# AdaLN transformer block, forward and backward: every DMA transpose replaced by TensorE transposes, dS of a group's second and fourth unit through the dP ring

## The chip, the cores and the metric

One core of a Trainium2 chip runs the whole program. The metric is the device time of one execution in microseconds. Three executions of the kernel before the change gave 2509.86, 2512.61 and 2517.3 us, so the median is 2512.61 us.

## The reference, cut to what matters

The function is one transformer block whose two layer norms are modulated by a conditioning vector, and the reference returns the output and the gradient of nine inputs.

```
mod = silu(c) @ w_mod                     # six rows: sa, ca, ga, sb, cb, gb
h   = layernorm(x) * (1 + ca) + sa
q, k, v = (h @ wqkv), 32 heads of 16
p   = softmax(q k^T / 4);  o = p v        # 2048 x 2048 scores for each head
x1  = x + ga * (o @ wo)
h2  = layernorm(x1) * (1 + cb) + sb
out = x1 + gb * (relu(h2 @ w1 + b1)^2 @ w2 + b2)
grads = vjp(out)(grad_out)                # for x, wqkv, wo, w1, b1, w2, b2, c, w_mod
```

There are 2048 tokens, 512 features, 1792 hidden units, all inputs in bf16. In the backward pass each head needs dP = dO v^T, dS = p * (dP - rowsum), and from dS the gradients dK = dS^T q and dQ = dS k. With keys on one axis of a tile and queries on the other, one of these two products needs dS as it was made and the other needs it turned. That turned dS is the subject of the larger part of the change.

## The kernel before, in words

Time runs through five stages, and the names below are those of the code.

**Forward attention** (`phase_fwd`, 0 to about 980 us). The outer loop runs over `order`: four chunks of 512 queries, eight groups of four heads, two pairs in a group, so 64 pairs (`n`), and inside each over 16 blocks of 128 keys (`kb`). One step makes two score tiles of 128x512 on TensorE (line 388), one exp of 128x1024 on ScalarE (line 391), and eight small products with V (line 322). Beside that, a `Background` object deals out other TensorE work in small portions. A generator yields a number, which is the cost of what it has just issued in units of one 512-column matmul, or a pair such as `("wait", 3)`, which makes the next three steps deal out nothing, so that another engine has time to finish. `step(rate)` gives about 1.2 units per step in the first chunk of queries and 1.14 in the later ones. `until(mark)`, `take` and `drain` run the generators at once: there the waits are passed over. During the first chunk of queries the background is `gen_qkv` (projections for the next head groups, with `gen_fm` and `gen_vt`, which also bring Q, K and V into token-major or padded layouts by DMA transposes at lines 646 and 705); during the other three it is `gen_mlp` (output projection, the MLP forward and backward of the preceding chunk of 512 tokens, then `gen_do`), with DMA transposes at lines 1176, 1178, 1201, 1248 and 1332, and those of the weights at 1139, 1152 and 1153. `bg.until(g + 1)` and `bg.until(-(g + 1))` in the first chunk, and `bg.until(f"fc2_{SC - 2}")` at line 410 after the loop, force what is not yet done.

**Last chunk and weight gradients** (`last_chunk`, about 983 to 1166 us). The last 512 tokens go through the MLP without attention beside it, and `gen_dw1` and `gen_dw2` make the gradients of w1 and w2 in 14 blocks (`ft`) each. `turned` fetches a block of 12 x 128 columns turned, by DMA (lines 946 and 950), three blocks ahead with four buffers.

**Backward attention** (`attn_bwd`, about 1166 to 2382 us). There are 16 pairs of heads, for each four chunks `c` of 512 keys, for each 16 blocks `ib` of 128 queries: 1024 units. Four units are a group, with `i` from 0 to 3. A unit makes two score tiles (line 1608) in the PSUM ring `st` and two dP tiles (line 1522) in the ring `dp`; each ring has three buffers of one bank. The matmuls of both use 64 rows of the array each, and on opposite halves. ScalarE turns scores into `pu` by exp (line 1611), VectorE multiplies dP by `pu` into `ds` (line 1526). In 160 of the 256 groups the second half of unit `i == 1` is copied to SBUF by ScalarE (line 1540) and multiplied by GpSimd (line 1541) instead. `kv` (line 1459) takes dK and dV from `ds` and `pu` in four column tiles; `dq` (line 1484) takes dQ from `dsT`, the turned dS. `dS` (line 1543) starts, when the fourth unit of a group is done, one DMA transpose of the whole group, at line 1549, on SyncE's queue; for one group in four `turn_ds` (line 1556) first turns four of its 32 blocks on TensorE, and ScalarE copies those out. `dq` runs more than eight pending steps behind (`len(pendq) > 2 * G`). In this stage the order of TensorE, SyncE and GpSimd is the order of the code. GpSimd issues the loads of the next group's tensors (line 1597).

**Last products** (`phase6`, about 2382 us to the end). dK, dQ and dV of all heads are multiplied with the weights; `load_a` (line 1733) turns two token blocks of three tensors by three DMA transposes for each of eight steps.

Of the kernel before, what the change touches and what calls it, by code (L numbers as in the profile page):

```python
# [19 lines left out]
P = 128  # L20
# [85 lines left out]
class K:  # L106
# [160 lines left out]
    def phase_fwd(self):  # L267
# [145 lines left out]
        nc.sync.dma_start_transpose(self.gT_l[:], self.io["grad_out"][0, S - 512:, :])  # L413
# [210 lines left out]
    def gen_fm(self, ps, t, g, s0, dst=None, masked=None):  # L624

        nc = self.nc
        DT, NQ = self.DT, self.NQ
        eb = self.qkv_eb
        pt = ps.tile([P, 512], F32, name="pps")
        for kt in range(DT):  # L630
            nc.tensor.matmul(pt[:], lhsT=self.wpads[t][:, kt, g, :] if g else self.wpad0[t][:, kt, :], rhs=self.xm1T[:, kt, s0:s0 + 512],
                             start=(kt == 0), stop=(kt == DT - 1))
            if kt < DT - 1:
                yield 1
        if dst is None:
            ev = eb.tile([P, 512], BF16, name="ev_fm")
            dst = ev[:]
        nc.vector.tensor_copy(dst, pt[:])
        if masked:
            for j in range(4):  # L640
                (nc.scalar.copy if j == 1 else nc.vector.tensor_copy)(masked[j][32 * j:32 * j + 32, :], ev[32 * j:32 * j + 32, :])
        nc.sync.dma_start((self.QTq_d, self.KTq_d)[t][g, :, s0:s0 + 512], dst)

        def token_major():
            tm = eb.tile([P, 4, 4, 32], BF16, name="ev_tm")
            nc.sync.dma_start_transpose(tm[:].rearrange("p s j e -> p s (j e)"), dst)
            if t:
                nc.gpsimd.dma_start(self.ktm_d[g, :, s0:s0 + 512], tm[:].rearrange("p s j e -> p (s j e)"))
                return
            tmc = eb.tile([P, 4, 4, DH], BF16, name="ev_tmc")  # L650
            nc.gpsimd.tensor_copy(tmc[:], tm[:, :, :, 0:DH])
            w = 4 * DH
            nc.gpsimd.dma_start(self.qtm_d[g, :, s0 // P * w:(s0 // P + 4) * w],
                                tmc[:].rearrange("p s j d -> p (s j d)"))

        if self.late is None:
            token_major()
        else:
            self.late.append(token_major)
        yield 1  # L660

    def gen_qkv(self, kp):
# [3 lines left out]
        for g in range(1, NQ):  # L666
# [8 lines left out]
            if 3 < g <= 3 + self.DT:  # L675
                wt = self.qkv_eb.tile([P, 3 * self.DT, P], BF16, name="wm_t", bufs=1)
                nc.sync.dma_start_transpose(wt[:], w[:])
                nc.gpsimd.dma_start(self.WmT_d[g - 4], wt[:].rearrange("p n k -> p (n k)"))
# [14 lines left out]
    def gen_vt(self, s0):  # L693
# [4 lines left out]
        for k in range(4):  # L698
# [6 lines left out]
            nc.sync.dma_start_transpose(vT[:, :, k * P:(k + 1) * P], vp[:].rearrange("p g j e -> p (g j e)"))  # L705
            yield ("wait", 1)
        nc.gpsimd.dma_start(self.VTq_d.rearrange("g p s -> p g s")[:, :, s0 * P:(s0 + 4) * P], vT[:])

# [53 lines left out]
    def last_chunk(self, bg, O_b, x0s, o32):  # L762
# [11 lines left out]
        tps = self.open_pool("tps", bufs=2, space=PSUM)  # L774
# [25 lines left out]
        bg.take(4)  # L800
        stats = mk.tile([P, 4, 6], F32, name="stats")
# [137 lines left out]
    def turned(self):  # L939

        nc, ST, FT = self.nc, self.ST, self.FT
        lasts = []

        def get(pool, src, src_d, ft):
            r = pool.tile([P, ST - 4, P], BF16, name="tm_blk", bufs=4)
            nc.sync.dma_start_transpose(r[:], src_d[ft, :, :(ST - 4) * P])
            if ft % 4 == 0:
                n = min(4, FT - ft)
                t = pool.tile([P, 4, 4, P], BF16, name="tm_l", bufs=2)
                nc.sync.dma_start_transpose(t[:, :n].rearrange("p f s k -> p (f s) k"),  # L950
                                            src[:, ft:ft + n, :].rearrange("p f k -> p (f k)"))
                lasts.append(t)
            return [r[:, st, :] for st in range(ST - 4)] + [lasts[-1][:, ft % 4, i, :] for i in range(4)]

        return get

    def gen_dw1(self, sb, xh2, duT):
# [22 lines left out]
        dus = [turned(sb, duT, self.duT_d, ft) for ft in range(3)]  # L980
# [3 lines left out]
        for ft in range(FT):  # L984
            if ft + 3 < FT:
                dus.append(turned(sb, duT, self.duT_d, ft + 3))
# [37 lines left out]
    def gen_dw2(self, sb, g_tm, aT, tb):  # L1024
# [15 lines left out]
        load(0)  # L1040
        load(1)
        yield 0
        load(2)
        for ft in range(FT):
            if ft + 3 < FT:
                load(ft + 3)
# [74 lines left out]
    def gen_weights_1(self):  # L1121
# [17 lines left out]
        nc.sync.dma_start_transpose(self.wogaT[:].rearrange("p a b c -> p (a b) c"), wo[:].rearrange("p a b -> p (a b)"))  # L1139

    def gen_weights_2(self):
# [10 lines left out]
        nc.sync.dma_start_transpose(self.W2gbT[:].rearrange("p a b c -> p (a b) c"), w2[:].rearrange("p a b -> p (a b)"))  # L1152
        nc.sync.dma_start_transpose(self.W1mT[:].rearrange("p a b c -> p (a b) c"), w1[:].rearrange("p a b -> p (a b)"))
# [14 lines left out]
    def gen_mlp(self, sc, O_b):  # L1168
# [5 lines left out]
        x_v, g_v, out_v = tm_v(io["A_x"][0]), tm_v(io["grad_out"][0]), tm_v(io["out_0"][0])  # L1174
        OT = mk.tile([P, 4, DT, P], BF16, name="fT", bufs=2)
        nc.sync.dma_start_transpose(OT[:].rearrange("p a b c -> p (a b) c"), O_b[:].rearrange("p a b -> p (a b)"))
        gT = mk.tile([P, DT, 512], BF16, name="fT", bufs=2)
        nc.sync.dma_start_transpose(gT[:], io["grad_out"][0, s0:s0 + 512, :])
        yield ("wait", 9 if sc else 14)
# [21 lines left out]
        nc.sync.dma_start_transpose(xhT[:].rearrange("p a b c -> p (a b) c"), xh[:].rearrange("p a b -> p (a b)"))  # L1201
# [30 lines left out]
        for k in range(4):  # L1232
# [15 lines left out]
            nc.sync.dma_start_transpose(dxT[:], dxb[:])  # L1248
# [40 lines left out]
    def gen_do(self, sc, k, dxT, pads=None, o32=None):  # L1289
# [42 lines left out]
        nc.sync.dma_start_transpose(self.dOTq[:, :, c0:c0 + P], dOpad[:].rearrange("p g j e -> p (g j e)"))  # L1332
# [98 lines left out]
    def attn_bwd(self):  # L1431
# [18 lines left out]
        pend, pendq, turnq, two = [], [], [], []  # L1450
# [92 lines left out]
        def dS(u):  # L1543

            (T, g, jp, c, ib, kvT, pu, dsg, i, grp) = u
            pend.append((T, g, jp, c, ib, kvT, pu, dsg[:, i]))
            if i == G - 1:
                dsT, n = grp
                nc.sync.dma_start_transpose(dsT.rearrange("p (b k) -> p b k", k=P)[:, n:, :],
                                            dsg[:].rearrange("p i a k -> p (i a k)")[:, n * P:])  # L1550
# [4 lines left out]

        def turn_ds(dsg, grp, skip, late):

            dsT = next(t for t in dT_free if not late or t is not own)
            dT_free[:] = [t for t in dT_free if t is not dsT]
            grp.extend((dsT, 0 if skip else 4))  # L1560
            if skip:
                return
            tp = stp.tile([P, 4, P], BF16, name="st")
            for b in range(4):
                nc.tensor.transpose(tp[:, b, :], dsg[:, 0, 0, b * P:(b + 1) * P], self.ident[:])
            nc.scalar.copy(dsT[:, 0:4 * P], tp[:].rearrange("p b k -> p (b k)"))
# [5 lines left out]
        for g in range(NQ):  # L1572
            for jp in range(2):
# [16 lines left out]
                for c in range(SC):  # L1590
                    c0 = 512 * c
                    for ib0 in range(0, ST, G):
# [6 lines left out]
                        for i in range(G):  # L1599
# [21 lines left out]
                            elif i % 2 == 0 and len(pendq) > 2 * G:  # L1621
                                for _ in range(4 if end else 2):
                                    dq(pendq.pop(0))
                            if i == 2:
                                turn_ds(dsg, grp, no_turn(c, ib), end and m > 2)
            T = Tn
        with tc.manual_schedule(engines=ALL):
# [5 lines left out]
            dS(last)  # L1633
            while len(pend) > 2:
# [50 lines left out]
    def phase6(self):  # L1685
# [47 lines left out]
        def load_a(i):  # L1733
            s2 = order[2 * i]
            dqT = wk.tile([P, 3, 2, DT, P], BF16, name="dqT", bufs=3)
            for t in (1, 2, 0):
                nc.sync.dma_start_transpose(dqT[:, t].rearrange("p s n k -> p (s n) k"),
                                            parts[t][:, s2:s2 + 2, :].rearrange("p s d -> p (s d)"))
# [227 lines left out]
```

## Time and profile before

| what | value |
|---|---|
| median of three executions | 2512.61 us |
| the profiled execution, its own time | 2500.32 us |
| its span | 2498.5 us |
| granted TensorE clock, mean | 0.998 |
| busy: TensorE, ScalarE, VectorE, GpSimd | 2410.2, 2283.1, 1695.0, 753.5 us |
| busy: TensorE's weight load | 1061.6 us |
| DMA, mean | 182 GB/s; 1,293,547 packets, 1,236,948 of them under 512 B |

In the tables of the profile, a row is a group of instructions of one source line on one engine, with its output, its inputs, their shapes, the number of instructions, the busy time, the mean duration of one, and the idle time before it. A busy TensorE is not a full one: a matmul of 512 columns shows about 380 ns from its start to its end, while the starts of two that follow each other lie about 220 ns apart. The mean duration of a ScalarE or VectorE instruction also overlaps with that of its neighbour, so the busy time divided by the count is the better price.

### The profile page before, as it was taken

Reading aid. Unit: us, or ns where it says so; the run is one execution under the profiler, and the core shown is the slowest. Engines: PE = TensorE matmul, PEld = TensorE weight load, DVE = VectorE, ACT = ScalarE, POOL = GpSimd, SP = SyncE. Lnnn points to the kernel's source line nnn. Section 1 sums busy time; section 2 is a strip of 40 time slices with the busy share of each in tenths; the row PEclk is TensorE's granted clock in tenths of the full one; section 3 lists DMA queues with packets and bytes.
Section 4 is the critical chain, followed back from the end, with each engine's and each line's share of the span. In section 5 each row is a group of like instructions: output and inputs, shape, how many; then the busy total and the mean of one; then the engine's idle time right before and its main releaser. Section 6 shows DMA issues by size and latency. Waiting matters only on the chain.

```text
span 2498.5 us, 67897 instructions
## 1 busy us (share of the span) xinstructions
PE 2410.2 (96%) x26211; PEld 1061.6 (42%) x26439; DVE 1695.0 (68%) x3487; ACT 2283.1 (91%) x3757; POOL 753.5 (30%) x1337
## 2 busy tenths in 40 slices
PE   8999999999999999999999999999999999999998
PEld 4555555555555555583233332333333333333343
DVE  6222322422332343576999999999999999999957
ACT  7999999999999997534999999999999999999945
POOL 2344531220131022245222323322333222322223
PEclk9999999999999999999999999999999999999999
DMA  4589661541243045499999999999999999999997
GB/s 166 135 179 208 169 125 47 132 100 40 92 114 98 23 123 147 110 199 216 232 235 233 232 227 231 237 234 231 230 235 239 234 230 236 234 233 236 238 217 192
DMA packets 1293547, 454.13 MB, mean 182 GB/s; under 512 B 1236948, under 2 KB 1261398, under 8 KB 1293222
## 3 DMA queue, kind: packets, MB, share of 16 engines
q1 hardware_dynamic: 1252422, 344.68, 71.8%
q0 software_dynamic: 38720, 104.04, 13.9%
q8 instruction: 207, 3.39, 0.6%
q10 hardware_dynamic: 2080, 1.05, 0.2%
q14 instruction: 118, 0.97, 0.1%
HBM read 75.83 MB, written 64.49 MB: 56 GB/s over the span
## 4 chain that ended last, share of the span: by engine, by line
PE 49%; ACT 35%; DMA 7%; issue 5%; DVE 3%; POOL 1%; SPq 1%; ACTq 0%; DVEq 0%; POOLq 0%
ACT pu L391 26%; PE st L1608 17%; PE acckv L1459 8%; ACT pu L1611 6%; DMA dsT<-ds 5%; PE accq L1484 5%; PE st L388 4%; PE dp L1522 2%; PE accbank L322 2%; PE dps L1050 2%; PE dp L1659 1%; PE st L1754 1%; ACT csq L1540 1%; PE pps L1237 1%; DVE ds L1526 1%
## 5 line engine op out<-in xcount | busy, mean ns | idle before, releaser
L1526 DVE TENSOR_TENSOR ds<-dp,pu 128x512 bf16<-128x512 f32 x1888 | 1166.0, 682 | 34.6 <-PE dp L1522 19.1
L1611 ACT ACTIVATE pu<-st 128x512 bf16<-128x512 f32 x2048 | 1073.8, 666 | 34.7 <-PE st L1608 21.3
L391 ACT ACTIVATE pu<-st 128x1024 bf16<-128x1024 f32 x992 | 912.1, 1077 | 4.2 <-PE st L388 3.7
L388 PE MATMUL st<-QTm,KTq 128*128 128x512 bf16 x1859 | 560.9, 377 | 27.1 <-ACT pu L391 6.1
L322 PEld LDWEIGHTS <-pu 128*128 128x128 bf16 x8192 | 346.7, 96 | 236.1 <-issue 3.0
L1522 PE MATMUL dp<-kvm,q 64*128 64x512 bf16 x1024 | 365.0, 384 | 2.0 <-DVE ds L1526 0.7
L322 PE MATMUL accbank<-Vaug,pu 128*128 128x17 bf16 x8192 | 357.4, 171 | 8.3 <-ACT Vaug L522 1.1
L1522 PE MATMUL dp<-kvm,dOTg 64*128 64x512 bf16 x1024 | 363.6, 383 | 0.3
L1608 PE MATMUL st<-kvm,q 64*128 64x512 bf16 x1024 | 349.4, 382 | 5.4 <-ACT pu L1611 0.2
L1608 PE MATMUL st<-kvm,QTg 64*128 64x512 bf16 x1024 | 348.1, 381 | 6.5
L1541 POOL TENSOR_TENSOR ds<-csq,pu 128x512 bf16<-128x512 f32 x128 | 147.2, 1150 | 627.0 <-ACT csq L1540 553.6
L388 PEld LDWEIGHTS <-KTq 128*128 128x128 bf16 x1984 | 188.4, 96 | 176.9 <-issue 124.8
L1459 PE MATMUL acckv<-ds,Qg 128*16 128x512 bf16 x1024 | 176.2, 382 | 0.3
L1459 PE MATMUL acckv<-pu,q 128*16 128x512 bf16 x1024 | 176.3, 383 | 0.0
L1459 PE MATMUL acckv<-ds,q 128*16 128x512 bf16 x1024 | 176.2, 383 | 0.0
L1459 PE MATMUL acckv<-pu,dOg 128*16 128x512 bf16 x1024 | 176.0, 382 | 0.0
L302 POOL DMA_DIRECT2D QTm<-QTq_d x124 | 63.1, 511 | 341.5 <-PE st L388 320.0
L1608 PEld LDWEIGHTS <-q 64*128 64x128 bf16 x1024 | 67.0, 94 | 163.5 <-issue 150.6
L1608 PEld LDWEIGHTS <-QTg 64*128 64x128 bf16 x1024 | 67.1, 94 | 160.6 <-issue 145.7
L329 DVE RECIPROCAL rl<-accbank 128x4 f32<-128x4 f32 x128 | 22.9, 179 | 158.3 <-PE accbank L322 158.2
L1522 PEld LDWEIGHTS <-q 64*128 64x128 bf16 x1024 | 88.8, 93 | 52.9 <-issue 43.3
L1522 PEld LDWEIGHTS <-dOTg 64*128 64x128 bf16 x1024 | 88.2, 93 | 52.9 <-issue 43.8
(390 smaller groups left out, 3055.1 us busy)
## 6 DMA issues: line engine op xcount, KB each, us to landing
KTq<-KTq_d POOLq DMA_DIRECT2D x24, 512.0 KB, 3.9
duT_d<-auT POOLq DMA_DIRECT2D x3, 1792.0 KB, 7.9
aT_d<-rT POOLq DMA_DIRECT2D x3, 1792.0 KB, 11.5
KTq_d<-KTq SPq DMA_DIRECT2D x32, 128.0 KB, 2.1
QTq_d<-ev_fm SPq DMA_DIRECT2D x32, 128.0 KB, 4.3
ktm_d<-ev_tm POOLq DMA_DIRECT2D x32, 128.0 KB, 2.5
VTq_d<-vT POOLq DMA_DIRECT2D x4, 1024.0 KB, 6.3
dx<-dx_d SPq DMA_DIRECT2D x16, 256.0 KB, 4.6
```

What stands on the lines that cost most here:

```text
L302: nc.gpsimd.dma_start(QTm[j][32 * j:32 * j + 32, :], self.QTq_d[g, 32 * j:32 * j + 32, 512 * qc:512 * (qc + 1)])
L322: nc.tensor.matmul(acc[:, a, sub, :], lhsT=pu[:, a, sub * P:(sub + 1) * P], rhs=Vaug[:, kb, h, :], start=(kb == 0 and a == 0 and sub == 0) ...
L388: nc.tensor.matmul(stt[:, a, :], lhsT=KT[:, kb * P:(kb + 1) * P], rhs=QTm[2 * jp + a][:], start=True, stop=True)
L391: nc.scalar.activation(pu[:], stt[:], ACT.Exp, scale=self.scale)
L1050: nc.tensor.matmul(pt[:], lhsT=a[st], rhs=g_tm[:, st, :], start=(st == 0), stop=(st == ST - 1))
L1459: nc.tensor.matmul(acckv[r:r + DH, :], lhsT=T[n][:, ib, col:col + DH], rhs=src[:, a, :], start=(ib == 0), stop=(ib == ST - 1))
L1484: nc.tensor.matmul(accq[r:r + 32, o:o + 256], lhsT=T["K"][:, 4 * c + sub, col:col + 32], rhs=v[:, r // 32 % 2 * 2:r // 32 % 2 * 2 + 2, 4 * ...
L1522: nc.tensor.matmul(dp[:], lhsT=T["dOT"][rd, ib * P:(ib + 1) * P], rhs=masked["VT"][a][rd, 512 * c:512 * (c + 1)], start=True, stop=True)
L1526: nc.vector.tensor_tensor(dsg[:, i, a], dp[:], pu[:, a, :], ALU.mult)
L1541: nc.gpsimd.tensor_tensor(dsg[:, i, 1], f[:], pu[:, 1, :], ALU.mult)
L1608: nc.tensor.matmul(stt[:], lhsT=T["QT"][rs, q], rhs=masked["KT"][a][rs, c0:c0 + 512], start=True, stop=True)
L1611: nc.scalar.activation(pu[:, a, :], stt[:], ACT.Exp, scale=self.scale)
```

## The change

No DMA transpose is left. `gen_turn` does the same with TensorE: up to eight blocks of 128x128 go as transposes into one PSUM bank, and one copy brings them to SBUF. `turn_now` runs it in one go.

```
    def gen_turn(self, dst, src, n, pool=None, name="pps", copies=None):
        nc = self.nc
        for b0 in range(0, n, 8):
            m = min(8, n - b0)
            pt = (pool or self.mps).tile([P, 8, P], BF16, name=name)
            for i in range(m):
                nc.tensor.transpose(pt[:, i, :], src[:, (b0 + i) * P:(b0 + i + 1) * P], self.ident[:])
                if i == 3:
                    yield 1.5
            (copies or [nc.vector.tensor_copy])[b0 // 8 % len(copies or [0])](dst[:, b0:b0 + m, :], pt[:, :m, :])
            yield 1.5
```

In the forward pass the generators now yield from it, with a wait ahead of it in several places (`("wait", 3)` in `gen_vt`, and before the turns of `xh` and `dxb`; `("wait", 4)` before that of `dOpad`; `("wait", 1)` in `gen_fm`). The chunk's `grad_out` is loaded as it is (`g_s`) and turned. All these copies are VectorE's.

In the backward attention `dS` only queues the unit, and the loop turns it at the end of the next unit's step:

```
         def dS(u):
             (T, g, jp, c, ib, kvT, pu, dsg, i, grp) = u
             pend.append((T, g, jp, c, ib, kvT, pu, dsg[:, i]))
+            tq.append(u)
+
+        def turn_unit(u):
+            ...
+            self.turn_now(dsT.rearrange("p (b k) -> p b k", k=P)[:, 2 * G * i:2 * G * (i + 1), :],
+                          dsg[:, i].rearrange("p a k -> p (a k)"), 2 * G, pool=(stp, dpp)[i % 2], name=("st", "dp")[i % 2],
+                          copies=[(nc.scalar.copy, nc.vector.tensor_copy)[i % 2]])
             if i == G - 1:
-                dsT, n = grp
-                nc.sync.dma_start_transpose(dsT.rearrange("p (b k) -> p b k", k=P)[:, n:, :],
-                                            dsg[:].rearrange("p i a k -> p (i a k)")[:, n * P:])
                 two.append(dsT)
...
-                            elif i % 2 == 0 and len(pendq) > 2 * G:
+                            elif i % 2 == 0 and len(pendq) > G:
...
-                            if i == 2:
-                                turn_ds(dsg, grp, no_turn(c, ib), end and m > 2)
+                            while len(tq) > 1:
+                                turn_unit(tq.pop(0))
```

Units with even `i` use a buffer of the `st` ring and ScalarE's copy, units with odd `i` a buffer of the `dp` ring and VectorE's copy. `turn_ds` and its four transposes are gone.

In the weight gradients `turned` loads a block plainly into one buffer (`tm_st`, `bufs=1`) and turns it one block later, in `flush`, in the PSUM pool `tps` with two buffers, with copies by ScalarE and VectorE in turn; it now runs two blocks ahead instead of three. `last_chunk` turns its four blocks of `grad_out` with its own `turn`. In `phase6`, `load_a` does its three turns in the `st` ring, one copy by VectorE and two by ScalarE.

## The prediction

> **What bounds the kernel now.** I read the busy time by stage first, because the page's averages mix five stages. The stages are the opening, forward attention of the first 512 queries, that of the other 1536, last chunk and weight gradients, backward attention, last products. The columns after the length are the busy times of TensorE, its weight load, VectorE, ScalarE and GpSimd with their counts, then granted clock, DMA share and GB/s.
>
> ```profile
> 0.00:64.00 64.00, 55.34 (x514) 29.18 (x524) 41.96 (x108) 47.70 (x56) 19.23 (x39) 1.00 0.47 165
> 64.00:290.00 226.00, 212.88 (x2655) 123.36 (x2701) 58.02 (x154) 224.38 (x245) 106.79 (x189) 1.00 0.79 182
> 290.00:983.00 693.00, 668.92 (x8171) 377.91 (x8323) 222.06 (x659) 687.92 (x749) 151.87 (x244) 1.00 0.36 90
> 983.00:1166.00 183.00, 174.02 (x1507) 110.00 (x1517) 115.10 (x456) 72.77 (x170) 80.70 (x118) 0.99 0.80 186
> 1166.00:2382.00 1216.00, 1193.72 (x12845) 374.53 (x12845) 1176.29 (x1906) 1195.90 (x2430) 360.66 (x688) 1.00 1.20 232
> 2382.00:2498.50 116.50, 105.26 (x526) 46.64 (x532) 81.54 (x205) 54.44 (x109) 34.30 (x60) 0.98 0.84 203
> ```
>
> Backward attention takes 1216 us for 1024 units, 1.1875 us each. ScalarE is busy for 1195.90 (1.168 a unit) and VectorE for 1176.29 (1.149): both are full. In forward attention ScalarE alone is full. The other two stages hang on TensorE. Then the groups of the backward stage:
>
> ```profile
> L1526 DVE TENSOR_TENSOR ds<-dp,pu 128x512 bf16<-128x512 f32 x1888 | 1166.0, 682 | 34.6 <-PE dp L1522 19.1 <-ACT pu L1611 1.2 <-ACT junk L1540 0.8
> L1611 ACT ACTIVATE pu<-st 128x512 bf16<-128x512 f32 x2048 | 1073.8, 666 | 34.7 <-PE st L1608 21.3 <-PE dp L1522 9.3
> L1566 ACT COPY dsT<-st 128x512 bf16<-128x512 bf16 x52 | 31.3, 602 | 0.5 <-PE st L1565 0.2
> ```
>
> Next, who waits for the DMA transposes there. In the list of waits from 1200 to 2300 us it is one row:
>
> ```profile
> PE accq L1484 <- DMA dsT<-ds: 7.2, 11, 2.9
> ```
>
> So 7.2 us is about all that the transposes cost that stage (the chain's 5% for them is a route through a queue, with full engines beside it). Last, what a turn costs on TensorE and on the copying engines, from the turns that exist: four blocks inside the backward loop, eight blocks of the last chunk with what follows each, and the copies at line 783.
>
> ```profile
> 1700.77 0.40 PE L1565 MATMUL st<-ident,ds 128*128 128x128 bf16 x4
> 1701.10 0.39 PE L1608 MATMUL st<-kvm,QTg 64*128 64x512 bf16 x1
> ...
> 1039.94 0.61 PE L782 MATMUL tp<-ident,dOpad 128*128 128x128 bf16 x8
> 1040.38 1.03 PE L1299 MATMUL pps<-wogaT,dxT 128*128 128x512 bf16 x4
> ```
>
> ```profile
> L783 DVE COPY fT<-tp x4: 414/418/424, 983.2 to 997.6; 128x512 bf16<-128x512 bf16 x4
> L783 ACT COPY dOTq<-tp x4: 1003/1012/1012, 1040.8 to 1061.3; 128x1024 bf16<-128x1024 bf16 x4
> ```
>
> Starts of neighbours give the price: eight transposes take 0.44 us of TensorE, 0.055 each, and a change from them to the half-array score matmuls adds some 0.11 (0.33 for four).
>
> **Backward attention, the change's main part.** It removes 256 DMA transposes that nobody waits for, 256 TensorE transposes and 64 ScalarE copies, and adds 1024 x 8 = 8192 TensorE transposes, 512 copies of 128x1024 on ScalarE and 512 on VectorE.
>
> ScalarE: an exp of 128x512 shows 666 ns but 1073.8/2048 = 524 ns of busy time, so 142 ns overlap; the copy of 1012 ns costs about 0.86 and the removed one of 602 ns about 0.46. Floor: 1195.9 + 512 x 0.86 - 64 x 0.46 = 1607 us, 1.57 a unit.
>
> VectorE: no row shows a PSUM copy of 128x1024. The nearest is 128x512 from bf16 in 419 ns, while the same width from fp32 PSUM takes 690 (line 1225). The 271 ns between them are half of a one-per-cycle pass, which leaves a fixed part of 148 and gives 148 + 2 x 271 = 690 ns, less the overlap of 682 - 1166.0/1.888 = 64: 0.626 us. Floor: 1176.3 + 512 x 0.626 = 1497 us. The Trainium skill, "VectorE: DVE Perf Modes", in "Rules for kernel authors", tells one to accept the single rate with a PSUM source. By that rule the copy is 148 + 1084 - 64 = 1.17 us and the floor 1774, which would make VectorE the bound. Its own table of perf modes allows up to double for copies, and the 419 ns row says double; I take the row and keep the other end for the range.
>
> TensorE: in the timeline scores with their dP start 0.22 us apart, `kv` takes 0.215, two `dq` steps 0.23, and each change between half-array and column tiles adds 0.10. A group of four units has 8 x 0.22 + 4 x 0.215 + 4 x 0.115 = 3.08 us and 8 or 12 changes: 3.9 or 4.3 us, 1.02 a unit, hidden today under 1.17 of ScalarE. The turn adds 0.44 + 0.11; with the removed ones (0.33 per 16 units) that is 1.55 a unit, 1587 us. So TensorE, which had 14% of slack, stands level with ScalarE.
>
> Two waits come on top. First, the GpSimd half: in 160 groups (the counts of line 1541) the second half of unit 1 is copied by ScalarE and multiplied by GpSimd in 1150 ns. It is ready 0.55 + 0.2 + 1.15 = 1.9 us after the last exp of unit 2; TensorE reaches the turn of unit 1 after the scores and `kv` of unit 3, about 0.75 us after that exp. The turn then stands about 1.2 us at the head of TensorE's queue, and behind it wait the next scores. ScalarE has csq copy, turned copy and two exps queued (2.46 us), the next score is there at about 2.95, so 0.5 us is lost: 160 x 0.5 = 80 us. Before, `dS` was needed only by `kv`, two units later, and by the DMA. Second, three engines at 1.46 to 1.57 a unit are coupled through rings of three tiles, in which a turn now takes every fifth place. The stage loses 20 us to coupling now with one engine slack; I take 50 (3%). Bounds: 0 and 300.
>
> Sum: 1607 + 80 + 50 - 1216 = +521 us. GpSimd's loads land sooner on an empty DMA; nobody waited for them. `dq` starting at four pending steps instead of eight is free as long as turned tiles are ready a group earlier than needed; if not, TensorE waits as it did for the DMA, 7 us.
>
> **Transposes and the clock.** "TensorE: Matmul & The Clock Gate", part "PE-mode transpose", gives about 275 ns for a 128x128 turn in a kernel and says that turns don't count as activity for the full clock. At 275 ns a unit's turn is 2.2 us and the stage ends near 3.3 ms alone. The row says 0.055 at clock 1.00 (as in the stage from 1030 to 1064 us, which has such turns). I take the row. The clock half is a rival below: real matmuls still fill over 0.7 us of each unit.
>
> **Forward, first 512 queries (+50).** I counted what the generators yield. Before, `until` forces 6 units between steps there; afterwards 157 beyond these, because turns and the new waits (steps that deal out nothing) delay the list while the marks stay. Forced, the waits are passed over: a `gen_fm` is four matmuls (0.86), VectorE's cast (0.69 and 0.3 of signalling), four turns (0.3): 2.15 us, during which no score is made. ScalarE has two tiles ahead, 1.84 us. Four bursts of about 4.6 such calls cost 8.4 us each, eight small ones about 2: +50.
>
> **Forward, rest (+88).** In the loop itself a turn is charged 1.5 for four blocks, more than its 0.25 us; +5 for turns that stand on VectorE's chain. The plain load `g_s` has nine steps of 0.92 us to land in; without them its 3 us would show once a chunk. At the end line 410 finds 229 units undone where before there were none: all of the third chunk's MLP from the hidden layer on. Hidden layer 12.5 us, its derivative 14.5 (VectorE's 690 and 424 ns per block, overlapped), then four times 14 matmuls (3.0), the norm's backward chain (4.0: six operations of line 1273 to 1287 and a cast), turn (0.7), `gen_do` (0.86), its chain (3.9), turn (0.8), in TensorE's order one after the other, 13.2 us, with half of that for the first: 48, then 8.6 for the rest. Total 83 us, with ScalarE idle.
>
> **Last chunk and weight gradients (+52).** The drain has 31 units instead of 9: +5. `grad_out`'s 16 turns: +2. The 28 blocks turn 448 times, 448 x 0.062 = 28 us on a TensorE that shows 25.00 busy of 25.00 in dw1; every fourth block needs four PSUM tiles of two and waits for copies of 1.0 and 0.69 (8 x 1.5 = 12); the first load, now in TensorE's way, 4. The single `tm_st` buffer has a block's 4 us to land 384 KB, and loads of 512 KB land in 3.9: nearly covered; without cover 1 to 2 us a block, 28 to 56.
>
> **Last products (+20).** 192 turns, 192 x 0.062 = 12, and waits for ring places and copies at the two first calls and behind `dx`, 8.
>
> Together +521 + 50 + 88 + 52 + 20 = +731. The profiled execution took 2500.32 us (span 2498.5, 1.8 around it), so 3231; the median of the runs is 12.3 above it, so 3244.
>
> **The rivals.** (1) Packed to the floor: the stall on GpSimd and the coupling hide, the other stages cost half. +391 and 105 give 3010 for the median at the lowest; the case reaches from there to about 3110. For it speaks that ScalarE and VectorE both run at 97 to 98% now. (2) Lockstep: the turn's copy stands in a queue between exps, TensorE waits for the ring place. Two units then take scores 0.44, exp 0.67, turn 0.75, copy 1.01, second scores and exp 0.89: 3.76, 1.88 a unit, +709, and 1.3 times the rest: about 3500. For it speaks that no engine has slack to catch up. (3) The clock drops to half in the backward stage: the array's 0.77 + 0.44 us a unit come twice, 2.76 a unit, +1610: about 4330. (4) Not slower: the DMA's traffic stretches ScalarE and VectorE, and without it every exp is shorter. It decides from 731/2048 = 0.36 us of an exp's 0.524. The exp of forward attention speaks against it, at a DMA share of 0.87 and of 0.30:
>
> ```profile
> 150.00:230.00 80.00, 79.32 (x87) 1.00 0.87 189
> ...
> 500.00:700.00 200.00, 199.92 (x219) 1.00 0.30 81
> ```
>
> That is 0.912 us each at the high share and 0.913 at the low. Even at half of that an exp would save 0.07. (5) The change does nothing: excluded by the instruction order, which has 9680 transposes at `gen_turn` and no DMA transpose.
>
> **How the numbers follow.** The forecast has 0.52, (1) 0.24, (2) 0.19, (3) 0.03, (4) and (5) 0.02 together. The range reaches from near the floor, 3030, to just over the lockstep case, 3540, which leaves out the edge of (1), the upper part of (2), the clock and the rest: about 2 in 10. A slower VectorE copy (1774 as floor) lies inside. The runs before spread by 0.3%, so a change under that can't be told from none. Faster 0.01, same 0.01, slower 0.98.
>
> **What would show it.** Backward attention longer by about 520 us at 1.7 us a unit; the copy near 1.0 us on ScalarE and 0.69 on VectorE; TensorE's turns waiting for GpSimd's `ds`; DMA share there down from 1.20 to under 0.2; a stretch of about 80 us without exps before the last chunk; a dw1 block of about 5.5 us. Wrong would be: turns far over 0.06 us each, a granted clock under 0.95 in the stage, VectorE as the one full engine, or a backward stage outside 1600 to 1950 us.

## The result, and the profile after

The changed kernel takes 3248.57 us (median of four executions, 3241.86 to 3250.46) against 2511.24 us of the kernel before (four executions, 2507.23 to 2517.3). The ratio is 1.2929, with a 95% interval of 1.2895 to 1.2962. The forecast was 3244 us. The profiled execution took 3241.86 us, of which 3240.1 are its span, against 2498.5 before: 741.6 us more, where the prediction's parts summed to 731.

The busy times by stage come first again. The columns are the same as before: TensorE, its weight load, VectorE, ScalarE, GpSimd, then clock, DMA share and GB/s. The cuts are now set where the work changes: the first 512 queries, the other 1536, the forced end of forward attention, the last chunk with the weight gradients, backward attention, the last products.

```profile
64.00:338.00 274.00, 232.82 (x2859) 138.21 (x2908) 90.54 (x225) 206.22 (x224) 87.37 (x165) 0.99 0.23 76
338.00:1046.00 708.00, 671.29 (x8503) 396.31 (x8657) 205.06 (x587) 706.82 (x771) 148.88 (x235) 1.00 0.21 67
1046.00:1136.00 90.00, 59.27 (x276) 26.03 (x278) 59.21 (x152) 0.02 (x1) 20.67 (x33) 0.85 0.30 98
1136.00:1365.00 229.00, 209.94 (x1998) 138.83 (x2010) 129.15 (x494) 109.55 (x208) 80.87 (x119) 0.98 0.44 136
1365.00:3102.00 1737.00, 1683.03 (x20726) 790.84 (x20724) 1525.79 (x2416) 1677.15 (x2874) 358.82 (x683) 1.00 0.05 14
3102.00:3240.00 138.00, 123.02 (x773) 60.89 (x780) 88.72 (x216) 71.46 (x129) 37.31 (x66) 0.97 0.39 122
```

Three things are to be seen. Backward attention has grown to 1737 us, with TensorE busy for 1683 and ScalarE for 1677, and the DMA at a share of 0.05, where it had been 1.20 in 1216 us. A stage has appeared that was not there: from 1046 to 1136 us ScalarE does nothing, and the granted clock falls to 0.85. And the first 512 queries take 274 us with ScalarE busy for only 206. The same 223 exps in both kernels, asked for by the exp's line alone (ScalarE's busy time, clock, DMA, GB/s; the first row is of before, the second of after):

```profile
64.00:271.00 207.00, 205.19 (x223) 1.00 0.75 172
```

```profile
64.00:338.00 274.00, 206.01 (x223) 0.99 0.23 76
```

The exps cost the same. The 67 us are all waiting, and the list of waits of that stretch has nearly all of them in one row, thirteen waits with the longest of 11.8 us:

```profile
ACT pu L391 <- PE st L388: 66.3, 13, 11.8
```

The groups of backward attention in the changed kernel, which answer to those shown of before:

```profile
L1562 DVE TENSOR_TENSOR ds<-dp,pu 128x512 bf16<-128x512 f32 x1888 | 1226.0, 685 | 137.4 <-PE dp L1558 98.7
L1645 ACT ACTIVATE pu<-st 128x512 bf16<-128x512 f32 x2048 | 1116.5, 611 | 43.9 <-PE dp L1558 15.7
L720 ACT COPY dsT<-st 128x1024 bf16<-128x1024 bf16 x416 | 427.2, 1027 | 18.4 <-PE st L717 12.1
L720 DVE COPY dsT<-dp 128x1024 bf16<-128x1024 bf16 x416 | 286.5, 689 | 60.1 <-PE dp L717 49.7
```

VectorE's copy shows 689 ns (690 were worked out), ScalarE's 1.03 us. The exps' row has 1116.5 us instead of 1073.8, but most of that is counting and no cost. The busy time of a group takes off only what its own instructions overlap; where an exp overlaps a copy, both groups count the overlap, and there are now more such places. The nine groups of ScalarE in this stage sum to 1296 us before and 1815 after, while ScalarE as a whole was busy for 1194 and 1677: 102 and 139 us stand twice in the rows. The wait on the DMA for `dsT` is gone from the list of waits, and waits for GpSimd have come in at TensorE's turn. The two rows (1400 to 3050 us) show the same waits, once at the weight load and once at the matmul:

```profile
PEld L717 <- POOL ds L1577: 47.7, 122, 0.7
...
PE dp L717 <- POOL ds L1577: 26.8, 121, 0.5
```

The price of a unit's turn on TensorE, from the start of its eight transposes to that of the next scores, is 0.55 us, change of array shape included:

```profile
1999.87 0.62 PE L717 MATMUL st<-ident,ds 128*128 128x128 bf16 x8
2000.42 0.39 PE L1642 MATMUL st<-kvm,q 64*128 64x512 bf16 x1
```

Part by part, each difference between the two traces beside what was predicted. Backward attention is taken from the start of the first exp to that of the last: 1166.9 to 2375.8 us before, 1365.6 to 3100.7 after.

| part | predicted, us | measured, us |
|---|---|---|
| first 512 queries | +50 | 274 - 207 = +67 |
| other queries, in the loop | +5 | 708 - 710 = -2 |
| forced end of forward attention | +83 | 1046 to 1136, 2 before: +88 |
| last chunk, weight gradients | +52 | 229 - 184 = +45 |
| backward attention | +521 | 1735.1 - 1208.9 = +526 |
| last products | +20 | the rest of 741.6: about +17 |

In the second and third row, before counts 271 to 981 us for the loop and the 2 us to 983 for the forced end.

### The profile page after: what moved, and what is told of

It reads as the page before. It is cut to its first block, busy times and chain, and to the rows that moved or that the text cites. A ratio compares the mean times of both kernels' runs of the same rounds, so it can differ in the third digit from the quotient of the medians.

```text
span 3240.1 us, 86820 instructions
## 1 busy us (share of the span) xinstructions
PE 3034.6 (94%) x35635; PEld 1580.3 (49%) x35879; DVE 2140.4 (66%) x4195; ACT 2818.9 (87%) x4259; POOL 753.1 (23%) x1337
## 4 chain that ended last, share of the span: by engine, by line
PE 32%; issue 30%; ACT 24%; POOL 8%; DVE 5%; DMA 0%; POOLq 0%; DVEq 0%; ACTq 0%; SPq 0%
ACT pu L391 21%; PE st L1642 5%; POOL ds L1577 4%; PE dp L717 3%; DVE ds L1562 3%; PE st L388 3%; PE st L717 2%; PE acckv L1495 2%; PE dps L1024 1%; PE accbank L322 1%; PE dps L1080 1%; PE accq L1520 1%; PE pps L630 1%; PE dp L1695 1%; PE st L1790 1%
## 5 line engine op out<-in xcount | busy, mean ns | idle before, releaser
L1562 DVE TENSOR_TENSOR ds<-dp,pu 128x512 bf16<-128x512 f32 x1888 | 1226.0, 685 | 137.4 <-PE dp L1558 98.7
L1645 ACT ACTIVATE pu<-st 128x512 bf16<-128x512 f32 x2048 | 1116.5, 611 | 43.9 <-PE dp L1558 15.7
L391 ACT ACTIVATE pu<-st 128x1024 bf16<-128x1024 f32 x992 | 912.8, 1081 | 69.0 <-PE st L388 67.5
L717 PEld LDWEIGHTS <-ds 128*128 128x128 bf16 x8192 | 461.0, 98 | 334.4 <-issue 282.0
L720 ACT COPY dsT<-st 128x1024 bf16<-128x1024 bf16 x416 | 427.2, 1027 | 18.4 <-PE st L717 12.1
L717 PE MATMUL dp<-ident,ds 128*128 128x128 bf16 x4096 | 340.6, 221 | 29.7 <-POOL ds L1577 29.0
L1642 PE MATMUL st<-kvm,q 64*128 64x512 bf16 x1024 | 332.7, 383 | 9.8 <-ACT dsT L720 5.6
L1558 PE MATMUL dp<-kvm,q 64*128 64x512 bf16 x1024 | 337.6, 383 | 1.0 <-PE st L1642 0.7
L1558 PE MATMUL dp<-kvm,dOTg 64*128 64x512 bf16 x1024 | 337.5, 382 | 0.0
L720 DVE COPY dsT<-dp 128x1024 bf16<-128x1024 bf16 x416 | 286.5, 689 | 60.1 <-PE dp L717 49.7
L717 PE MATMUL st<-ident,ds 128*128 128x128 bf16 x4096 | 318.1, 221 | 0.1
```

What stands on the lines that cost most here:

```text
L391: nc.scalar.activation(pu[:], stt[:], ACT.Exp, scale=self.scale)
L717: nc.tensor.transpose(pt[:, i, :], src[:, (b0 + i) * P:(b0 + i + 1) * P], self.ident[:])
L720: (copies or [nc.vector.tensor_copy])[b0 // 8 % len(copies or [0])](dst[:, b0:b0 + m, :], pt[:, :m, :])
L1558: nc.tensor.matmul(dp[:], lhsT=T["dOT"][rd, ib * P:(ib + 1) * P], rhs=masked["VT"][a][rd, 512 * c:512 * (c + 1)], start=True, stop=True)
L1562: nc.vector.tensor_tensor(dsg[:, i, a], dp[:], pu[:, a, :], ALU.mult)
L1642: nc.tensor.matmul(stt[:], lhsT=T["QT"][rs, q], rhs=masked["KT"][a][rs, c0:c0 + 512], start=True, stop=True)
```

## The experiments

In what follows "the stage" is backward attention, from the start of its first exp to that of its last, as above. A run with a single time was executed once. The stage repeats well: where its code was the same, it took 1735.1, 1734.2 and 1735.3 us (after, runs 1 and 11) and 1208.9 and 1208.1 us (before, run 2). Runs 6 to 9 leave out part of the turned dS.

**1. Backward attention alone changed.** The kernel before, with the new `dS`, `turn_unit`, `tq` and the `gen_turn` they need; everything else turns by DMA.

```
-                nc.sync.dma_start_transpose(dsT..., dsg...)     # dS, and turn_ds
+            tq.append(u)                                        # dS
+                            while len(tq) > 1:
+                                turn_unit(tq.pop(0))
```

> The kernel before, with the change in backward attention alone: its turns by TensorE, all other turns by DMA as before. If the parts add up as the prediction has it, the backward stage takes 1737 us against 1216 before (the trace of after shows about 1735) and the run 2511 + 521 to 526 = 3032 to 3037 us. Rival, the DMA traffic of the forward stages or the late start of the backward one plays a part in the growth: the stage would differ from that of after by over 20 us.

Measured: 3035.03 us, stage 1734.2 us.

**2. All but backward attention changed.** The kernel after with those hunks taken back.

```
-                            while len(tq) > 1:
-                                turn_unit(tq.pop(0))
+                            if i == 2:
+                                turn_ds(dsg, grp, no_turn(c, ib), end and m > 2)
```

> The kernel after, with backward attention as before (dS by DMA). The rest of the change alone: the prediction's parts give 50 + 88 + 52 + 20 = 210, so 2721 us; the trace of after says 68 - 2 + 88 + 45 + 17 = 216, so 2727 us. A backward stage of 1216 us is expected unchanged. Rival: removing the other DMA transposes relieves the DMA queue in the backward stage, then the stage is shorter than 1205 us.

Measured: 2719.01 us, stage 1208.1 us. The parts add up: 3035 - 2511 and 2719 - 2511 are 524 and 208, 732 together of 737. The stage is neither longer nor shorter for what happens ahead of it (1734.2 and 1735.1; 1208.1 and 1208.9), so relief of the DMA queue from the other turns brought it nothing.

**3. Every turn half a step later.** No instruction is added; the turn stands behind the first score tile of the next step.

```
                                 if a == 0 and len(tq) > 1:
                                     turn_unit(tq.pop(0))
...
-                            while len(tq) > 1:
-                                turn_unit(tq.pop(0))
```

> The kernel after, with each unit's turn moved from the end of one step to behind the first score tile of the next, so that GpSimd has about 0.75 us more until TensorE needs its half of ds. No work is added or removed. Theory (the turn stands waiting for GpSimd in 160 groups, priced at 0.5 us each): TensorE's waits for GpSimd's ds go from some 75 us to under 20 and the backward stage gets 50 to 80 us shorter, 3170 to 3200 us in all. Rival (ScalarE is the bound at 1677 busy of 1737, the wait is hidden in slack): the waits go and the time stays within 15 us of 3248.

Measured: 3242.76 us, stage 1731.6 us. TensorE's waits for GpSimd are gone from the list, and only 3.5 us came of it. But TensorE was now busy for 1731.64 of 1737 us, 49 more than after: the turn splits each score pair, so changes of shape were added. The run could not tell whether these held the time or something else did.

**4. No GpSimd half.**

```
         def off(c, ib):
-            return odd(c, ib) or (c > 1 and ib // G == 2)
+            return False
```

> The kernel after without the GpSimd half: VectorE multiplies all of ds (160 products more, 160 x 0.62 = 99 us), ScalarE makes 160 copies less (160 x 0.52 = 83 us). Theory (stall on GpSimd plus coupling at a level of three engines): stall gone, ScalarE at about 1590 busy, VectorE at about 1625, stage about 1670, run about 3180. Rival (VectorE has no room either): the stage stays at 1735 or gets longer, because VectorE's 99 us show.

Measured: 3187.51 us, stage 1678.5 us, 56.6 less than after. VectorE was busy for 1611.95 us, 86 more than after, and had room for it. ScalarE lost 65 us of busy time, and the stage lost about as much, which looked like ScalarE setting the pace. Runs 7 and 9 show that this reading was wrong.

**5. Only unit 1 one step later.** In groups with a GpSimd half the turn of unit 1 is made together with that of unit 2.

```
-                            while len(tq) > 1:
+                            while tq and len(tq) > (2 if tq[0][8] == 1 and off(tq[0][3], tq[0][4]) else 1):
```

> The kernel after, in which only the turn of unit 1 of a group that uses GpSimd waits one step longer, and is then made together with that of unit 2; all others stand where they were. Unlike the half step, this adds no change between array shapes. Theory A (the stall on GpSimd costs wall time: 0.35 us shown at TensorE, 0.5 priced, 160 times): stage 1735 - 50 to 80 = 1655 to 1685 us, run 3170 to 3200. Theory B (ScalarE's work sets the pace, TensorE's wait lies in its slack): within 15 us of 3248. In the half step the wait went and 3.5 us came of it, but there some 0.1 us of TensorE a unit may have been added.

Measured: 3253.72 us (four executions), ratio to before 1.2963 (1.2905 to 1.3021), stage 1741.4 us. Taking away TensorE's wait for GpSimd brought nothing, without any added change of shape. The list of waits (1400 to 3050 us) shows why. Another wait stands in its place, for the ring place of a turned tile that ScalarE has not yet copied. It was there 31 times in the kernel after, and now comes 121 times for the tiles in `dsT` and 30 times for those in `keep`, once in nearly each of the groups with a GpSimd half. The waits of TensorE's matmuls for GpSimd and ScalarE together are as long as they were: 41.4 us after, 41.0 here.

```profile
PE st L1642 <- ACT dsT L720: 33.0, 121, 0.6
...
PE st L1642 <- ACT keep L720: 8.0, 30, 0.6
```

In the timeline of this kernel it looks like this. ScalarE has the copy for GpSimd (line 1576) and then the turned tile of unit 0 (line 720), 1.37 us from the start of one to the start of the next exp. Neither frees a score for it to work on, and the turned tile holds the third buffer of `st`:

```profile
2001.25 0.59 ACT L1576 COPY csq<-dp 128x512 f32<-128x512 f32 x1
...
2001.72 1.04 ACT L720 COPY dsT<-st 128x1024 bf16<-128x1024 bf16 x1
...
2002.62 2.11 ACT L1645 ACTIVATE pu<-st 128x512 bf16<-128x512 f32 x4
2002.81 0.37 PE L1642 MATMUL st<-kvm,q 64*128 64x512 bf16 x1 [0.17 <-ACT dsT L720]
```

**6. Half of the turns.**

```
+            n_turn, n_copy = part or (m, m)
-            for i in range(m):
+            for i in range(n_turn):
...
+                copy(dst[:, b0:b0 + m, :].rearrange("p (r b) k -> p r b k", r=2),
+                     pt[:, :n_turn, :].unsqueeze(1).to_broadcast([P, 2, n_turn, P]))
```

> The kernel after with four instead of eight transposes per unit in backward attention; the copies keep their 1024 columns and read the four turned blocks twice, so half of the turned dS is left out and replaced by the other half. TensorE has 0.22 us a unit less, 225 in all; ScalarE and VectorE do the same work. If TensorE alone set the pace: stage 1735 - 225 = 1510. If ScalarE does: not under its busy time of 1677 less what it lost by waiting, so 1650 to 1690. Three engines at a level (the prediction): 1660 to 1690.

Measured: 3144.62 us, stage 1634.4 us: 100.7 less, of some 225 us taken from TensorE by the price of a transpose. That is under all but the first of the expected figures, so none of the three readings fits. The row shows ScalarE full in TensorE's place:

```profile
1371.00:3007.00 1636.00, 1539.38 (x16640) 612.30 (x16642) 1507.03 (x2422) 1619.48 (x2875) 358.29 (x683) 0.99 0.05 14
```

**7. Half of ScalarE's copies.**

```
+            n_copy = min(m, n_copy)
-            (copies or [...])[...](dst[:, b0:b0 + m, :], pt[:, :m, :])
+            (copies or [...])[...](dst[:, b0:b0 + n_copy, :], pt[:, :n_copy, :])
...
+                          n_copy=(4, 8)[i % 2],          # turn_unit
```

> The kernel after with ScalarE copying four of the eight turned blocks of the even units, so that the other four blocks of those units are left out (they stay zero); all transposes and VectorE's copies stay. ScalarE has 512 x 0.43 = 220 us less. If ScalarE alone set the pace: stage 1735 - 220 = 1515. If TensorE stands right behind it at 1587 (the prediction): 1600 to 1650. If TensorE set the pace already: within 15 us of 1735.

Measured: 3232.29 us, stage 1720.7 us. ScalarE's busy time fell by 204 us, and the stage by 14.4. In the row of that stage it is TensorE that stays full:

```profile
1369.00:3091.00 1722.00, 1678.19 (x20717) 778.24 (x20716) 1528.82 (x2419) 1473.40 (x2874) 357.85 (x682) 1.00 0.05 14
```

So ScalarE doesn't set the pace of the changed stage. The third expectation came true.

**8. Both halves.** Edits 6 and 7 together, `part=(4, 4)` for even units and `(4, 8)` for odd ones.

> Both of the former together: four transposes in every unit, ScalarE's copy of the even units four blocks wide, VectorE's copy of the odd ones as wide as it was; half of the turned dS is left out. TensorE has 225 us less, ScalarE 220. The prediction's floors are then 1387 for ScalarE, 1362 for TensorE and 1497 for VectorE (1526 busy in the trace of after): VectorE binds and the stage takes 1530 to 1580 us, so more is won than by either alone and less than by their sum. If the parts simply added up, the two single results tell the sum.

Measured: 3066.43 us, stage 1557.6 us: 177.5 less, where the two alone gave 100.7 and 14.4. It lies in the expected 1530 to 1580, but not for the reasons given: the gain is more than the sum of the two, and it is TensorE and not VectorE that is full.

```profile
1369.00:2928.00 1559.00, 1536.20 (x16632) 555.14 (x16631) 1477.71 (x2420) 1450.24 (x2875) 357.47 (x682) 1.00 0.05 15
```

With TensorE relieved, ScalarE's copies count (76.8 us); with TensorE full, they don't (14.4).

**9. Edits 5 and 7 together.** Each brought almost nothing alone.

> The kernel after with two edits together that each brought almost nothing alone: the turn of unit 1 in groups with a GpSimd half one step later (takes away the wait for GpSimd), and ScalarE copying four of eight blocks of the even units (shortens the wait for the ring place behind ScalarE's two copies in a row; half of the even units' turned dS is left out). Theory: TensorE sets the pace, at 1.545 us a unit in even groups and 1.63 in odd ones by the timeline of after, 1626 us, and each of the two waits stands in for the other; with both away the stage takes 1640 to 1670 us, 65 to 95 less than after. Rival: the two gains only add (16 us less and 5 more): 1720 to 1730.

Measured: 3186.09 us, stage 1671.5 us: 63.6 less, where the sum of the single results is 8 (14.4 less and 6.3 more). The two waits stand in for each other. The stage ended 1.5 us over the theory's upper edge, about 45 us above TensorE's own 1626.

**10. A complete version of the same.** Edit 5, and VectorE copies the turned tile of unit 0 in the groups with a GpSimd half.

```
-                          copies=[(nc.scalar.copy, nc.vector.tensor_copy)[i % 2]])
+                          copies=[nc.vector.tensor_copy if i % 2 or (i == 0 and off(c, ib)) else nc.scalar.copy])
```

> A complete kernel made from the same reading: unit 1's turn one step later in the 160 groups with a GpSimd half, and in those groups VectorE copies the turned tile of unit 0, so that ScalarE has no second copy behind the csq copy. ScalarE 160 x 0.86 = 138 us less, VectorE 160 x 0.62 = 100 more (1626 busy). Theory: both waits gone, stage 1650 to 1690, run 3165 to 3205. Rival: VectorE, now as full as TensorE, takes over as the wait: stage at or above 1715, run above 3228.

Measured: 3168.11 us (3165.99 to 3169.74, four executions), ratio to before 1.2606 (1.2569 to 1.2643), stage 1659.3 us. That is 75.8 us of the stage without leaving anything out, as theory had it. The stage's row now shows TensorE alone near the whole of it:

```profile
1371.00:3025.00 1654.00, 1640.29 (x20659) 778.74 (x20659) 1590.69 (x2565) 1533.24 (x2704) 355.24 (x679) 1.00 0.05 14
```

VectorE at 1591 did not take over. The waits of TensorE's matmuls for GpSimd and ScalarE, 41.4 us after, are down to 4.6 (1400 to 3050 us).

A rival to the second wait is that ScalarE's whole load held the stage once GpSimd's wait was gone. Runs 9 and 10 speak against it: run 9 takes 226 us from ScalarE, spread over all groups (it leaves half of each copy), and gains 64; run 10 takes 144, and only in the groups with a GpSimd half, and gains 76. No run relieves ScalarE in the other groups alone.

**11. A turn charged less.**

```
                 if i == 3:
-                    yield 1.5
+                    yield 1.0
...
-            yield 1.5
+            yield 1.0
```

> The kernel after, with four blocks of a turn charged 1.0 unit instead of 1.5 in the background's account (they take 0.25 us, a unit is 0.22); no work is added or removed. Theory (work forced at the marks and at the end of forward attention costs 67 + 88 us, because the list is not through in time): some 50 units less are forced at the end and as many in the first chunk of queries, so 35 to 55 us less, 3195 to 3215 us. Rival (TensorE is full in the loop, so what is dealt out there slows the exps by as much): 3235 to 3260.

Measured: 3224.78 us, 24 less than the median of after (17 less than its profiled execution), between the two expectations. The last exp of forward attention starts 7.6 us earlier and backward attention 18.0, so 10.4 us were won at the forced end. The timelines show where. From the start of the last exp to the first matmul behind the hidden layer, after has 16 transposes and 56 hidden-layer matmuls, 15.9 us in all; this run has 19 of these matmuls and 4.3 us. The serial chain behind them stays. In the first 512 queries the exps waited 8 us less for scores (59.5 against 67.5 over the whole of forward attention), where the expectation had as many units saved as at the end. By a count of what the generators yield, the units forced there fall only by 13. That the waiting steps hold the list back, and not the charge, follows from that count alone; no run separates the two.

**12. The kernel before, all of dS by DMA.**

```
         def no_turn(c, ib):
-            return ib // G > 0
+            return True
```

> The kernel before without its four transposes per fourth group: all of dS by DMA. ScalarE, the full engine of that stage, has 64 copies less, 64 x 0.46 = 29 us. Theory (ScalarE sets the pace there, the DMA is covered): 15 to 29 us less than before, a ratio of 0.988 to 0.994. Rival (the DMA queue, at a share of 1.20, is at its limit, and dQ waits for turned tiles): the same or slower, by up to 30 us.

Measured: 2543.9 us (four executions), ratio to before 1.0116 (1.0078 to 1.0153), 33 us more than the kernel before beside it; the profiled executions have 1250.7 us in the stage instead of 1208.9. The theory failed and the rival came true, a little beyond its 30 us. ScalarE's busy time did fall, to 1185 us, but from 1200 to 2300 us TensorE's waits for turned tiles rose from 7.2 us (11 times) to 30.9 (35 times):

```profile
PE accq L1484 <- DMA dsT<-ds: 30.9, 35, 2.8
```

So the four transposes on TensorE in one group of four were worth more than they cost. Keeping the DMA just covered is the likely reason; the row has 24 of the 42 us, and the rest was not followed.

None of these runs points to a version that beats the kernel before: both parts of the change cost time by themselves (runs 1 and 2), and the fastest complete version with all turns on TensorE is run 10.

## Why the prediction was right, point by point

**The cost of a turn** was right: 0.055 us for a transpose, and copies that show 0.69 us on VectorE and 1.03 on ScalarE. As a price on ScalarE, 0.86 was a little low: in the timeline of run 5 the next exp starts 0.90 us after the copy (2001.72 to 2002.62). At the two places where a rule of the Trainium skill was weighed against a row, the row held. The 275 ns of "TensorE: Matmul & The Clock Gate", "PE-mode transpose", would have given over 3 ms for the stage. Its remark that turns don't count for the full clock is not tested here: the granted clock was 1.00 through a stage with 8192 turns, but other matmuls stand between them. The single rate with a PSUM source in the rules of "VectorE: DVE Perf Modes" is given there for elementwise work on a matmul's output; the copy ran as that page's table for copies allows, with 270 ns more for 512 columns more (689 against 419 ns).

**Backward attention, +521 predicted, +526 measured.** The size was right, and the term on which the sum was built was not the one that sets the pace. The prediction started from ScalarE's floor of 1607 us and called TensorE level with it at 1587. ScalarE's floor was good: 1619 us busy in run 6, where it is full. TensorE's was too low, in part by a slip: 0.02 us a unit were taken off for the removed transposes, which the 1.02 had not contained; without that it is 1608. In the timeline of after, steps of TensorE that wait for nothing take 1.545 us a unit in even groups and 1.63 in odd ones, 1626 us. So TensorE leads, by about 1%. Run 7 shows that 204 us less of ScalarE give 14, run 6 that 225 less of TensorE give 101, until ScalarE holds the stage.

That 521 came so near to 526 is partly luck. By these runs the sum is about 1626 for TensorE, 76 for the two waits and 33 for coupling, where the prediction had 1607, 80 and 50. The errors of the other parts, from -7 to +17 us, also cancel for the most part.

**The stall on GpSimd, 80 us.** The place was named rightly (the turn of unit 1, with the scores queued behind it), and the size of what is lost in these groups fits run 10, 76 us. But the step took it for one wait. Taken away alone (run 5), it was replaced by the wait for the ring place behind ScalarE's two copies, and only both together gave it back (runs 9 and 10). The prediction had ScalarE's csq copy, turned copy and two exps as a stock that covers the wait; they were a second wait of nearly the same length. Run 4 removed both at once, and for that reason looked like a proof of the first. What it did not settle, how the 57 us divide between them, runs 9 and 10 don't settle either, since each of the two waits alone is worth almost nothing.

**Coupling, 50 us.** With both waits gone, run 10 stands 33 us and run 9 45 us above TensorE's 1626, so the term was somewhat high.

**First 512 queries, 50 predicted, 67 measured.** The mechanism was right: bursts forced at the marks, in which no score is made. Both sizes were too low: the four long ones cost 8.0 to 11.8 us, 40.9 together, where 33.6 were worked out, and seven short ones 3.2 to 3.7, 24.4 together, where there were to be eight of 2.

**Forced end, 83 predicted, 88 measured.** The trace has the chain as worked out: after the matmuls of a block TensorE waits 3.77 us for VectorE's norm chain and, four matmuls later, 3.42 us for `dOpad`; one block takes 13.8 us, where 13.2 were predicted:

```profile
1090.39 0.40 PE L717 MATMUL pps<-ident,dxb 128*128 128x128 bf16 x4 [3.77 <-DVE dxb L1278]
1090.62 1.03 PE L1334 MATMUL pps<-wogaT,dxT 128*128 128x512 bf16 x4
1095.07 1.01 PE L717 MATMUL pps<-ident,dOpad 128*128 128x128 bf16 x8 [3.42 <-DVE dOpad L1360]
1095.87 4.57 PE L1271 MATMUL pps<-W1mT,auT 128*128 128x512 bf16 x14
...
1104.21 0.40 PE L717 MATMUL pps<-ident,dxb 128*128 128x128 bf16 x4 [3.77 <-DVE dxb L1278]
```

The 14 matmuls of line 1271 show 4.57 us here from the first start to the last end. The first such group of this stretch, at 1074.56 us, shows 3.19, as such a group does in the last chunk of the kernel before. The difference is the clock. Of this line alone (TensorE, its weight load, clock, DMA share, GB/s) the first group, then the two parts of the later one:

```profile
1074.56:1077.58 3.02, 3.02 (x14) 1.27 (x13) 1.00 0.00 0
...
1095.87:1098.43 2.56, 2.56 (x6) 0.91 (x7) 0.50 0.25 86
1098.43:1100.28 1.85, 1.85 (x9) 0.74 (x7) 0.94 0.00 0
```

Six matmuls start 0.43 us apart at a granted clock of 0.50, and the others 0.22 apart once it is back. From 1081.6 us on, after a first wait of 3.78 us, the clock stood at 0.50 for about half of the stretch, in pieces of 3.4 and 6.8 us. In three groups of 14 this costs 4.2 us, and in the turns beside them about 1 more, as much as the 88 us are over the 83 (which should have been 82, as three and a half blocks of 13.2 are 46 us and not 48). The prediction had no term for the clock in this stretch.

**Weight gradients and last products**, 52 and 20 predicted, 45 and 17 measured. Loads into the single `tm_st` buffer landed in 3.5 and 3.3 us (the profile's median), within a block's 4 us, so the cover held nearly: TensorE waited ten times for them, 6.5 us in all.

**What was ruled out** stayed out. The exps of forward attention got no shorter at a DMA share of 0.23 instead of 0.75 (206.01 us for 223 against 205.19). That the exps of backward attention show 611 ns instead of 666 is no relief from the DMA: in run 6, at the same DMA share of 0.05, they show 722.

## What to carry to other kernels

Price work moved off the DMA on every engine that it lands on, and add the occupancies: here the DMA transposes had cost 7 us of waiting in their largest stage, and their replacement put 0.55 us a unit on TensorE and about 0.45 on ScalarE, which had 14% (by the prediction's count) and 2% to spare. When a wait is taken away and nothing is won, look for the one that stood behind it before concluding that it cost nothing; two edits that were worth almost nothing each were worth 64 us together. And a list of background work that is dealt out by charges and waiting steps is paid for where it is forced: what does not get through in time runs with its dependences bare, and here at a lower clock as well.

## What the runs showed of the hardware that was not expected

The DMA turns of the kernel before were nearer to their limit than the 7.2 us of waits suggested: with 256 blocks more of the 8192 moved to them the kernel took 33 us longer, and the stage 42 us in the profiled executions (run 12).

The duration that an exp of 128x512 shows is not its price, and in these runs it went with how full ScalarE is: 666 ns before, 611 after, where ScalarE waits now and then, and 722 in run 6, where it is full again at the same number of copies. The spacing hardly moves: counted from the traces, an exp starts 477 ns (before), 494 (after) and 489 (run 6) after the exp ahead of it, as the median of those that overlap.

A stretch in which TensorE waits over 3 us again and again ran at a granted clock of 0.50 for about half of its time, and a matmul of 512 columns then took 0.43 us instead of 0.22.
